# Duo attention and a weighted sum of experts: keys head by head, expert weights in halves, first products earlier

## The chip, the cores and the metric

The kernel runs on one core of one Trainium2 chip. A core has TensorE (PE in the profile; its weight loads are PEld), VectorE (DVE), ScalarE (ACT), GpSimd (POOL) and SyncE (SP). Each takes its own instructions in order; they wait for each other through semaphores. DMA queues are filled from SP, ACT and POOL. The metric is the device time of one execution in microseconds, the median over runs.

## The reference

Eight heads of attention over 4 batches of 768 positions, then four experts over the 3072 rows that come out. Three heads (0, 2, 6) see all earlier keys ("retrieval"); five (1, 3, 4, 5, 7) see the first 4 keys and the last 64 ("streaming").

```python
scores = scale * np.matmul(q, k.transpose(0, 1, 3, 2))
stream_keep = causal & (is_sink | in_win)        # n_sink 4, window 64
mask = np.where(retr, causal, stream_keep)
a = softmax(np.where(mask, scores, -1e9))
x = matmul(a, v)                                 # to [N = 3072, D = 512]
p = domain_probs / (domain_probs.sum(-1, keepdims=True) + 1e-09)
for e in range(E):                               # E = 4, F = 1024
    h = np.maximum(x @ w1[e], 0.0)
    out += p[:, e:e + 1] * (h @ w2[e])
```

## The kernel before

**Stages.** Attention goes in 8 groups of 384 positions: group g is batch g // 2, half g % 2. What a group gives lies transposed in `xT[g]` (128 x 4 x 384: four quarters of the 512 inputs). The experts go over 24 token tiles of 128 rows. Tiles 0 to 2 (group 0) and then tile 3 take the plain way (`plain_steps`): for each expert, layer 1 makes 8 feature tiles, each a sum of four products (one for each quarter of the inputs, in the order 1, 0, 2, 3), which ACT takes out of PSUM with Relu (L1161); layer 2 makes for each token tile a sum of 8 products with `w2sb` (L1169), which DVE takes out times the probability (L1181, L1185). The other 20 tiles go in pairs (`pair_steps`) with Winograd's scheme, which needs sums of the weights and of the inputs; the sums of the inputs (`x_sum`) lie in the part of the key buffer that the windows of the later batches leave free.

**Order.** All engines' orders are written out by hand. `attention(0, 0)` runs first and alone. Then `moe_steps` yields steps, and after each one a plan decides by a running count whether the next steps of the following attention group are to be put in. `plan[1]` says from when group 1 is put in, in units of the plain work of one expert on group 0 (`UNIT`). Semaphore waits between instructions are put in by the layer that records them.

**Group 0's attention.** In it PE transposes keys and queries of a pair of heads (L619), DVE copies the keys into `kR` (retrieval, L645) or `kS` (streaming, L661, and the four first keys into every tile, L669), PE makes the scores (L736, biases L748), ACT the exponentials (L754), PE the values (L799, L863, and for the pairs 1, 5 and 3, 7 L905), and ACT and DVE divide by the sums (L914, L915, L918, L884, L828). The order is: transposes of heads 0, 1; scores 0, 1; transposes of 4, 5; values 0; scores 4, 5; transposes of 2, 3; values 1, 5; scores 3; transposes of 6, 7; and so on. `warm_up` puts matmuls on zeros where PE would wait; `WARM` says how many.

**Streaming keys.** `kS` holds 8 tiles of 96 keys with room for 128, for 5 heads. Before, the order within a partition is half, tile, head, key (`c t s x`). In later batches it holds 7 windows per head instead (`windows(kSf)`, L281), and what lies behind them holds `x_sum`. The two halves are zeroed at the start, the first by DVE, the second by POOL (both L371).

**POOL's start.** POOL builds masks, requests some of the values, casts values to 16 bits (L432), waits until the queries have landed (`landed`, L552), requests expert 0's first weights (`load_w1`, L327: two requests, one for each half of the partitions), casts again, requests expert 0's second weights (`load_w2`, L349), casts, zeroes the second half of the retrieval and of the streaming keys, fills in ones, and goes on with the next weights and with group 1's keys, queries and values. Requests of POOL are counted on eight semaphores in turn, so each waits for the eighth before it to land.

**PSUM.** `bank()` deals out four buffers in turn for scores, transposes and layer 1 (`pA`); `pO` has two for layer 2, and `pV` two.

Of the kernel before, what the change touches and what calls it, by code (L numbers as in the profile page):

```python
# [11 lines left out]
FP32 = mybir.dt.float32  # L12
# [7 lines left out]
def kernel(  # L20
# [42 lines left out]
    DMP = DM // P  # L63
    FTP = F // P
    NTILE = N // P
    G = B * NCH
# [5 lines left out]
    SH = [h for h in range(H) if not RETR[h]]  # L72
# [5 lines left out]
    NT = S // TK  # L78
    TC = CH // TK
# [3 lines left out]
    WT = 7  # L83
# [14 lines left out]
    gp = nc.gpsimd  # L98


    def bank():
        return pA.tile([P, 512], FP32, name="pA", bufs=4)
# [20 lines left out]
    kSf = pers.tile([P, NT * NSH * P], FP16, name="kS")  # L123
    vSf = pers.tile([P, NT * NSH * P], FP16, name="vS")

    kS = kSf.rearrange("p (c t s x) -> p c t s x", c=NCH, t=TC, s=NSH)
    vS = vSf.rearrange("p (c t s x) -> p c t s x", c=NCH, t=TC, s=NSH)

    def windows(x):

        return x[:, 0 : WT * NSH * P].rearrange("p (t s x) -> p t s x", t=WT, s=NSH)
# [36 lines left out]
    def half(u):  # L168
        return slice(u * D, (u + 1) * D)
# [8 lines left out]
    def key_tile(b, c, h, t):  # L178

        i = b % 2  # L180
        if RETR[h]:
            return kR[i][:, t // 3, RH.index(h), t % 3, :]
        if b:
            return windows(kSf)[:, t, SH.index(h), :]
        return kS[:, t // TC, t % TC, SH.index(h), :]

    def v_tiles(b, c, h):
# [90 lines left out]

    def keys_to_windows(b, c, part):

        x = windows(kSf)  # L281
        for r, n0, hp0, n in [((1, 0, 0, 2), (1, 3, 2, 2), (0, 2, 2, 1))[part]]:
            r = half(r)
            src = kT[r, hp0 : hp0 + n, P - WO + NS :]
            step = src.ap[1][0]
            src = bass.AP(
                src.tensor, src.offset, [src.ap[0], [step, n], [WQ, WT], [1, P - NS]]
            )
            dst = x[r, :, n0 : n0 + n, :].rearrange("p t n x -> p n t x")
            nc.vector.tensor_copy(out=dst[:, :, :, NS:P], in_=src)  # L290
            if c == 0:
                src = kT[r, hp0 : hp0 + n, P : P + NS]
                src = src.rearrange("p n (t x) -> p n t x", t=1)
                nc.vector.tensor_copy(
                    out=dst[:, :, :, 0:NS], in_=src.to_broadcast([D, n, WT, NS])
                )
        if part == 2 and b * NCH + c + 1 < G:
            nc.vector.tensor_copy(out=kT[:, :, P - WO : P], in_=kT[:, :, CH + P - WO :])
# [22 lines left out]
                out=vS[0:NS, c, t, :, :], in_=vS[R0 : R0 + NS, 0, 0, :, :]  # L321
            )

    def load_w1(e, f0, f1):
        x = moe_w1[e].rearrange("(u c d) f -> u d c f", u=2, c=DMP)
        for u in range(2):
            gp.dma_start(  # L327
                out=w1sb[half(u), e * DMP : (e + 1) * DMP, f0:f1],
                in_=x[u, :, :, f0:f1],
            )  # L330
# [14 lines left out]

    def load_w2(e):
        x = w2sb[:, e * FTP : (e + 1) * FTP, :]
        if in_pairs(e):
            gp.dma_start(  # L349
                out=x.rearrange("p (m j) d -> p m (j d)", j=2),  # L350
                in_=moe_w2[e].rearrange("(m p j) d -> p m (j d)", p=P, j=2),
            )
            return
        gp.dma_start(out=x, in_=moe_w2[e].rearrange("(fo fi) d -> fi fo d", fi=P))


    ONES = 0.0078125 * (1.0 + 15360.0 * 2.0**-23)

# [2 lines left out]
    def fill(eng, ap, value):  # L361
        ap = ap.bitcast(FP32)
        if eng is nc.scalar:
            src = ones[0 : ap.shape[0], :]
            if len(ap.shape) == 3:
                src = src.rearrange("p (a b) -> p a b", a=1)
            elif len(ap.shape) == 4:
                src = src.rearrange("p (a b c) -> p a b c", a=1, b=1)
            eng.copy(out=ap, in_=src.to_broadcast(list(ap.shape)))
        else:  # L370
            eng.memset(ap, value)  # L371

    def zero(eng, t):
        fill(eng, t.rearrange("p a b x -> p (a b x)"), 0.0)
# [60 lines left out]
    for n, h in enumerate(ORDER0):  # L435
# [24 lines left out]
        out=probs,  # L460
# [8 lines left out]
    make_identity(nc, ident32)  # L469
    one_values(nc.vector, 0)  # L470
    zero(nc.vector, kR[0][:, 0, :, :, :])
    zero(nc.vector, kS[:, 0, :, :, :])
    nc.vector.tensor_copy(out=ident16, in_=ident32)


# [76 lines left out]
        gp.tensor_copy(out=seen, in_=x)  # L552

    def w1_of(e):
        return w1sb[D : D + 1, e * DMP, 0:1]


    def w2_of(e):
        return w2sb[0:1, e * FTP, 0:1]


    landed(q32[0:1, 0, 6, 0:1])
    load_w1(0, 0, F)
    cast_v(gp, (4, 2, 3, 6))
    load_w2(0)
    cast_v(gp, (7,))
    zero(gp, kR[0][:, 1, :, :, :])
    zero(gp, kS[:, 1, :, :, :])
    one_values(gp, 1)

    load_w1(1, 0, F)
    landed(w1_of(0))
    load_triples(k, k16, 0, 1, 0, HP)
    load_triples(q, qt16, 0, 1, 0, HP)
# [2 lines left out]
    landed(qt16[0:1, 0, 0, 0:1])  # L577
    load_triples(k, k16, 0, 1, HP, H)
    load_triples(q, qt16, 0, 1, HP, H)
    load_w1(2, 0, F)  # L580
# [6 lines left out]
    load_w1(3, 0, F)  # L587
    load_w2(3)
    assert E == 4
    mSf = mS.rearrange("p t x -> p (t x)")  # L590
# [5 lines left out]

    def mm_ns(cols):
        return cols / 2.4 + 2.5

    def attention(b, c):  # L600
        g = b * NCH + c
# [320 lines left out]
            later(scale, g)  # L922
            yield 800.0

        WARM = {("s", 0): 3, ("v", 1): 3, ("v", 3): 4, ("v", 2): 2, ("v", 6): 2}

        def both(a, bb):

# [11 lines left out]
        if first:  # L940
# [190 lines left out]
    def acc_of(nt):  # L1131
        n0 = 2 * FTP * CH + nt * 2 * DM if nt < 3 else 5 * KT * P - 2 * DM
        return hA[:, n0 : n0 + 2 * DM].bitcast(FP32)

    def plain_steps(nt0, tiles, e, tokens, n0):

        cols_n = tiles * P
        hs = hA[:, n0 : n0 + FTP * cols_n].rearrange("p (f x) -> p f x", f=FTP)
        require(nt0 // 3)
        x = tokens()  # L1140
        ahead = 4 if nt0 == 0 and e == 0 else 1
        for f0 in [0, *range(ahead, FTP)]:
            pss = {ft: bank() for ft in range(f0, f0 + (1 if f0 else ahead))}
            cts = (1, 0, 2, 3)

            def layer1(ft, n):
                ct = cts[n]
                nc.tensor.matmul(  # L1148
                    out=pss[ft][:, 0:cols_n],
                    lhsT=w1_tile(e, ct, ft),  # L1150
                    rhs=x[:, ct, :],
                    start=(n == 0),
                    stop=(n == DMP - 1),
                )

            for ft in pss:
                for n in range(DMP - 1):
                    layer1(ft, n)
            for ft, ps in pss.items():
                layer1(ft, DMP - 1)  # L1160
                nc.scalar.activation(  # L1161
                    out=hs[:, ft, :], in_=ps[:, 0:cols_n], func=AF.Relu
                )
                yield DMP * mm_ns(cols_n), 0.6
        for j in range(tiles):
            nt = nt0 + j
            ps_o = pO.tile([P, DM], FP32, name="pO", bufs=2)
            for ft in range(FTP):
                nc.tensor.matmul(  # L1169
                    out=ps_o,  # L1170
                    lhsT=hs[:, ft, j * P : (j + 1) * P],
                    rhs=w2sb[:, e * FTP + ft, :],
                    start=(ft == 0),
                    stop=(ft == FTP - 1),
                )
                if ft == FTP // 2 - 1:
                    yield FTP // 2 * mm_ns(DM), 1.4
            p_ap = p_sb[:, nt, e : e + 1]
            if e == 0:
                acc[nt] = acc_of(nt)  # L1180
                nc.vector.tensor_scalar(  # L1181
                    out=acc[nt], in0=ps_o, scalar1=p_ap, scalar2=None, op0=ALU.mult
                )
            else:
                nc.vector.scalar_tensor_tensor(  # L1185
                    out=acc[nt], in0=ps_o, scalar=p_ap, in1=acc[nt],
                    op0=ALU.mult, op1=ALU.add,
                )
            if e == E - 1:
                nc.sync.dma_start(out=out[nt * P : (nt + 1) * P, :], in_=acc[nt])  # L1190
            yield FTP // 2 * mm_ns(DM), 1.4
# [46 lines left out]
        return scaled(e)[:, j * KH : (j + 1) * KH, i * P : (i + 1) * P]  # L1238

    second_set = set()  # L1240

    def x_sum(e, n):
# [31 lines left out]
    def pair_steps(nt0, nxt):  # L1274
# [446 lines left out]
```

## Time and profile before

| what | value |
|---|---|
| time, median of 3 runs | 376.75 us (376.45 to 376.91) |
| time of the profiled execution | 376.67 us |
| its span | 374.9 us |
| mean granted clock of PE | 0.998 |
| PE, DVE, ACT, POOL busy | 364.9, 278.1, 226.5, 113.7 us |
| expert 0's layer 1 on group 0 starts | 20.79 us |
| expert 0's layer 2 on group 0 | 26.23 to 31.57 us |
| tile 3's plain work starts | 72.73 us |

The span runs from the first instruction to the last; the time of the execution holds 1.77 us more around it. Rows of a timeline give start, duration, engine, line, operation, what is written and read, how many were merged, and in brackets how long the engine was idle before it and for what. Durations of merged rows reach from the first start to the last end. Rows of waits give the total, how often, and the longest. Line numbers are those of the kernel before.

### The profile page before, as it was taken

How to read it: one execution, taken by the hardware profiler on the slowest of the kernel's cores; microseconds unless marked ns; L12 is line 12 of the kernel's file. 1: busy time of each engine (PE TensorE's matmuls, PEld its weight loads, DVE VectorE, ACT ScalarE, POOL GpSimd, SP SyncE). 2: the span in 40 equal slices, each digit the busy share in tenths (PEclk: the TensorE clock that was granted, in tenths of full speed). 3: DMA queues.
4: the chain of work that ended last, by engine and by line, in shares of the span. 5: the costliest groups of instructions: out<-in, count | busy, mean ns of one | idle time of the engine just before them, and what ended most of it. 6: DMA issues, size and time to landing. Idle time of an engine off the chain costs nothing.

```text
span 374.9 us, 10308 instructions
## 1 busy us (share of the span) xinstructions
PE 364.9 (97%) x4219; PEld 310.2 (83%) x4219; DVE 278.1 (74%) x583; ACT 226.5 (60%) x471; POOL 113.7 (30%) x162
## 2 busy tenths in 40 slices
PE   7889899999999999999999999999999999999996
PEld 4645466678998988999989899988899998998995
DVE  5765867798687679868657858857768868979881
ACT  5644579547786785775776856774777361451630
POOL 8844573872067039015501640220000000000000
PEclk9999999999999999999999999999999999999999
DMA  9999999999799399989905990951220300300101
GB/s 179 193 211 206 195 195 182 180 201 97 111 104 163 79 99 139 156 96 85 187 2 73 166 152 12 140 121 12 72 68 2 111 7 2 114 3 14 43 3 58
DMA packets 122340, 39.65 MB, mean 106 GB/s; under 512 B 112192, under 2 KB 114820, under 8 KB 122292
## 3 DMA queue, kind: packets, MB, share of 16 engines
q0 software_dynamic: 82816, 19.01, 57.6%
q1 hardware_dynamic: 37876, 19.58, 23.5%
q8 instruction: 33, 0.54, 0.6%
q10 hardware_dynamic: 1600, 0.39, 0.5%
q14 instruction: 15, 0.12, 0.1%
HBM read 44.89 MB, written 6.34 MB: 137 GB/s over the span
## 4 chain that ended last, share of the span: by engine, by line
PE 85%; DVE 6%; DMA 5%; POOL 1%; issue 1%; ACT 1%; POOLq 0%; DVEq 0%
PE pO L1462 29%; PE pA L1282 21%; PE pO L1311 9%; PE pA L1148 7%; PE pO L1169 7%; PE pA L736 4%; DMA w1sb<-in_moe_w_dram 2%; PE pV L1311 2%; PE pA L1311 2%; PE pV L799 2%; DVE xs L1233 2%; PE pV L863 2%; DMA xT<-x_pair 1%; DMA hA<-in_v_dram 1%; DVE hA L1067 1%
## 5 line engine op out<-in xcount | busy, mean ns | idle before, releaser
L1462 PEld LDWEIGHTS <-hA 128*128 128x128 f16 x1104 | 104.8, 98 | 11.9
L1282 PE MATMUL pA<-xs,w1sb 128*128 128x256 f16 x768 | 97.1, 272 | 0.0
L1282 PEld LDWEIGHTS <-w1sb 128*128 128x128 f16 x768 | 71.7, 98 | 7.3
L1462 PE MATMUL pO<-w2sb,hA 128*128 128x256 f16 x640 | 76.8, 272 | 0.0
L754 ACT ACTIVATE es<-pA 128x384 f16<-128x384 f32 (+2 forms) x122 | 59.0, 512 | 27.4 <-PE pA L736 22.5
L1291 ACT ACTIVATE hA<-pA 128x512 f16<-128x512 f32 x96 | 57.2, 598 | 29.4 <-PE pA L1282 27.2
L306 POOL DMA_DIRECT2D vS<-in_v_dram x30 | 29.6, 988 | 111.7 <-PE pV L863 110.2
L1462 PE MATMUL pO<-tsb,hA 128*128 128x256 f16 x464 | 56.8, 272 | 0.0
L1233 DVE TENSOR_TENSOR xs<-xT,pB 128x1024 f16<-128x1024 f16 (+1 forms) x49 | 47.0, 977 | 2.9 <-DMA xT<-x_pair 2.9
L1067 DVE TENSOR_TENSOR hA<-hA 128x1024 f16<-128x1024 f16 x60 | 39.4, 685 | 0.6 <-PE pO L1462 0.3
L1161 ACT ACTIVATE hA<-pA 128x384 f16<-128x384 f32 (+1 forms) x64 | 22.2, 385 | 20.3 <-PE pA L1148 20.0
L1311 PEld LDWEIGHTS <-w1sb 128*128 128x128 f16 x512 | 31.3, 98 | 1.9 <-DVE xs L1067 0.6
L1148 PE MATMUL pA<-xT,w1sb 128*128 128x384 f16 (+1 forms) x256 | 30.4, 273 | 1.3 <-DMA w1sb<-in_moe_w_dram 1.2
L1169 PE MATMUL pO<-w2sb,hA 128*128 128x512 f16 x128 | 30.6, 379 | 0.0
L1482 ACT COPY s<-pO 128x256 f32<-128x256 f32 x31 | 11.6, 373 | 27.3 <-PE pO L1462 21.8
L1148 PEld LDWEIGHTS <-w1sb 128*128 128x128 f16 x256 | 19.4, 98 | 10.1 <-issue 1.7
L765 DVE TENSOR_TENSOR es<-es,mS 128x384 f16<-128x384 f16 (+1 forms) x40 | 13.8, 344 | 17.9 <-ACT es L754 17.9
L884 DVE TENSOR_TENSOR xT<-pV,rc 64x384 f16<-64x384 f32 x36 | 20.0, 555 | 8.3 <-ACT rc L881 7.7
L1328 DVE CUSTOM_DVE_ANT_0 hA<-pO,s 128x512 f16<-128x512 f32 x26 | 17.7, 688 | 9.8 <-PE pO L1311 8.5
L878 ACT ACTIVATE rc<-pV,eps 64x384 f32<-64x384 f32 x36 | 20.7, 576 | 6.6 <-PE pV L863 6.0
L1321 ACT COPY s<-pO 128x512 f32<-128x512 f32 x39 | 22.7, 587 | 3.2 <-PE pO L1311 3.0
L736 PE MATMUL pA<-qT,kR 128*128 128x128 f16 (+2 forms) x141 | 23.1, 261 | 0.7 <-DVE kR L645 0.7
(175 smaller groups left out, 520.3 us busy)
## 6 DMA issues: line engine op xcount, KB each, us to landing
pB<-p_rows SPq DMA_DIRECT2D x10, 512.0 KB
out_dram<-o SPq DMA_DIRECT2D x19, 256.0 KB
w1sb<-in_moe_w_dram POOLq DMA_DIRECT2D x8, 512.0 KB, 9.0
w2sb<-in_moe_w_dram POOLq DMA_DIRECT2D x4, 1024.0 KB, 11.3
vS<-in_v_dram POOLq DMA_DIRECT2D x30, 112.0 KB, 4.6
k_rows<-in_k_dram POOLq DMA_DIRECT2D x18, 128.0 KB, 5.0
q<-in_q_dram POOLq DMA_DIRECT2D x18, 128.0 KB, 6.0
out_dram<-hA SPq DMA_DIRECT2D x4, 256.0 KB
```

Source lines behind the costliest of these rows:

```text
L306: gp.dma_start(out=t[:, :, own_v(h)], in_=windows_of(v, b, h, c))
L736: nc.tensor.matmul(out=ps[:, o : o + nq], lhsT=key_tile(b, c, h, t), rhs=qTs[b, c][:, hp, q0 : q0 + nq], start=(n == 0 or not first), stop ...
L754: nc.scalar.activation(out=es[:, 0:cols], in_=ps[:, 0:cols], func=AF.Exp, scale=SC)
L1067: nc.vector.tensor_tensor(out=out, in0=a, in1=b, op=ALU.subtract)
L1148: nc.tensor.matmul(out=pss[ft][:, 0:cols_n], lhsT=w1_tile(e, ct, ft), rhs=x[:, ct, :], start=(n == 0), stop=(n == DMP - 1),)
L1169: nc.tensor.matmul(out=ps_o, lhsT=hs[:, ft, j * P : (j + 1) * P], rhs=w2sb[:, e * FTP + ft, :], start=(ft == 0), stop=(ft == FTP - 1),)
L1233: nc.vector.tensor_tensor(out=o, in0=xin, in1=pb.to_broadcast([P, DMP, n, P]), op=ALU.mult)
L1282: nc.tensor.matmul(out=ps[:, f * PC : (f + 1) * PC], lhsT=w1_tile(e, ct, f0 + f), rhs=xs[:, ct, :], start=(ct == 0), stop=(ct == DMP - 1),)
L1291: nc.scalar.activation(out=blocks[:, b0 : b0 + 2, k0 : k0 + 2, :].rearrange("p t f x -> p f t x"), in_=ps.rearrange("p (f t x) -> p f t x" ...
L1311: nc.tensor.matmul(out=ps[:, f * P : (f + 1) * P], lhsT=w_tile(e, w[:, ct, :], f), rhs=a[:, ct, :], start=(first and f == 0 and ct == 0), ...
L1321: nc.scalar.copy(out=kept[n], in_=ps)
L1462: nc.tensor.matmul(out=ps, lhsT=a[:, k, :], rhs=b(k), start=(first and k == 0), stop=(k == KT - 1), skip_group_check=not first,)
```

## The change

- The streaming keys lie head by head: the order within a partition is head, half, tile, key (`s c t x`). The windows of later batches are a view of the same order (`kW`), whose eighth tile of each head holds `x_sum` until all attention is done (`after_keys`), as two runs of 128 with other keys between; before the third last pair's second layer `require(G - 1)` asks for the attention to be finished, and from there on `x_sum` goes where it went before. The zero fill of a half is five runs (`zero_keys`).
- `load_w1` makes four requests (two quarters of the inputs, one half of the partitions each) in place of two, and `load_w2` two in place of one. What `landed` looks at lies in the last of them.
- Layer 1 of the plain experts makes the products of the first two quarters for four feature tiles ahead, for every expert on group 0 (before: for expert 0 alone, with three quarters ahead). Of expert 0 the first two feature tiles' first products are made in group 0's attention (`begin_products`), ahead of the values of heads 3 and 7, where four warm-up matmuls were.
- Layer 2 on group 0 goes over halves of the features: first half of tile 0, first half of tile 1, second half of 0, second half of 1, then both of tile 2.
- Group 1 is put in from 1.2 units on (before: 1.06).

```diff
-    kS = kSf.rearrange("p (c t s x) -> p c t s x", c=NCH, t=TC, s=NSH)
+    kS_rows = kSf.rearrange("p (s c t x) -> p c s t x", c=NCH, t=TC, s=NSH)
+    kS = kS_rows.rearrange("p c s t x -> p c t s x")
+    kW = kSf.rearrange("p (s t x) -> p t s x", s=NSH, t=NT)
...
-            return windows(kSf)[:, t, SH.index(h), :]
+            return kW[:, t, SH.index(h), :]
...
-        x = windows(kSf)
+        x = kW[:, 0:WT, :, :]
...
-    def load_w1(e, f0, f1):
+    def load_w1(e):
         x = moe_w1[e].rearrange("(u c d) f -> u d c f", u=2, c=DMP)
-        for u in range(2):
-            gp.dma_start(
-                out=w1sb[half(u), e * DMP : (e + 1) * DMP, f0:f1],
-                in_=x[u, :, :, f0:f1],
-            )
+        for c in range(0, DMP, 2):
+            for u in range(2):
+                gp.dma_start(
+                    out=w1sb[half(u), e * DMP + c : e * DMP + c + 2, :],
+                    in_=x[u, :, c : c + 2, :],
+                )
...
     def load_w2(e):
         x = w2sb[:, e * FTP : (e + 1) * FTP, :]
-        if in_pairs(e):
+        for n in range(2):
+            if in_pairs(e):
+                m = slice(n * FTP // 4, (n + 1) * FTP // 4)
+                gp.dma_start(
+                    out=x.rearrange("p (m j) d -> p m (j d)", j=2)[:, m, :],
+                    in_=moe_w2[e].rearrange("(m p j) d -> p m (j d)", p=P, j=2)[
+                        :, m, :
+                    ],
+                )
+                continue
+            m = slice(n * FTP // 2, (n + 1) * FTP // 2)
             gp.dma_start(
...
+    def zero_keys(eng, c):
+        fill(eng, kS_rows[:, c, :, :, :].rearrange("p s t x -> p s (t x)"), 0.0)
...
-    zero(nc.vector, kS[:, 0, :, :, :])
+    zero_keys(nc.vector, 0)
...
-        return w1sb[D : D + 1, e * DMP, 0:1]
+        return w1sb[D : D + 1, (e + 1) * DMP - 1, 0:1]
...
-    zero(gp, kS[:, 1, :, :, :])
+    zero_keys(gp, 1)
...
+    def begin_products(e, fts):
+
+        for ft in fts:
+            begun[0, e, ft] = bank()
+            layer1(begun[0, e, ft], e, ft, xT[0], (0, 1))
...
-        WARM = {("s", 0): 3, ("v", 1): 3, ("v", 3): 4, ("v", 2): 2, ("v", 6): 2}
+        WARM = {("s", 0): 3, ("v", 1): 3, ("v", 2): 2, ("v", 6): 2}
...
             yield from values(6)
+            begin_products(0, (0, 1))
             yield from values_pair(3, 7)
...
-        ahead = 4 if nt0 == 0 and e == 0 else 1
+        ahead = 4 if nt0 == 0 else 1
         for f0 in [0, *range(ahead, FTP)]:
...
+            for ft in range(f0, f0 + (1 if f0 else ahead)):
+                if (nt0, e, ft) in begun:
+                    pss[ft] = begun.pop((nt0, e, ft))
+                    continue
+                pss[ft] = bank()
+                layer1(pss[ft], e, ft, x, (0, 1))
+            if nt0 == e == f0 == 0:
+                for ft, ps in pss.items():
+                    layer1(ps, e, ft, x, (2,))
             for ft, ps in pss.items():
-                layer1(ft, DMP - 1)
+                layer1(ps, e, ft, x, (3,) if nt0 == e == f0 == 0 else (2, 3))
...
-        for j in range(tiles):
+        FH = FTP // 2
+        parts = [(j, n) for j in range(tiles) for n in range(2)]
+        if nt0 == 0:
+            parts = [(0, 0), (1, 0), (0, 1), (1, 1), (2, 0), (2, 1)]
+        sums_of = {}
+        for j, n in parts:
             nt = nt0 + j
-            ps_o = pO.tile([P, DM], FP32, name="pO", bufs=2)
-            for ft in range(FTP):
+            if n == 0:
+                sums_of[j] = pO.tile([P, DM], FP32, name="pO", bufs=2)
+            ps_o = sums_of[j]
+            for ft in range(n * FH, (n + 1) * FH):
...
     def x_sum(e, n):
 
+        if not after_keys:
+            return kW[:, WT, n * KH : (n + 1) * KH, :]
...
+        if nt0 == pairs[-3]:
+            require(G - 1)
+            after_keys.append(True)
...
-    plan = {1: (1.06 * UNIT, 3.5 * UNIT)}
+    plan = {1: (1.2 * UNIT, 3.5 * UNIT)}
```

More of the change, by code (lines that the diff above doesn't have):

```diff
@@ L124 @@
     vSf = pers.tile([P, NT * NSH * P], FP16, name="vS")
-    kS = kSf.rearrange("p (c t s x) -> p c t s x", c=NCH, t=TC, s=NSH)
+    kS_rows = kSf.rearrange("p (s c t x) -> p c s t x", c=NCH, t=TC, s=NSH)
+    kS = kS_rows.rearrange("p c s t x -> p c t s x")
+    kW = kSf.rearrange("p (s t x) -> p t s x", s=NSH, t=NT)
+    assert NT == WT + 1
     vS = vSf.rearrange("p (c t s x) -> p c t s x", c=NCH, t=TC, s=NSH)
@@ L347, in load_w2 @@
         x = w2sb[:, e * FTP : (e + 1) * FTP, :]
-        if in_pairs(e):
+        for n in range(2):
[9 more added lines that the diff above has]
+            m = slice(n * FTP // 2, (n + 1) * FTP // 2)
             gp.dma_start(
-                out=x.rearrange("p (m j) d -> p m (j d)", j=2),
-                in_=moe_w2[e].rearrange("(m p j) d -> p m (j d)", p=P, j=2),
-            )
-            return
-        gp.dma_start(out=x, in_=moe_w2[e].rearrange("(fo fi) d -> fi fo d", fi=P))
+                out=x[:, m, :],
+                in_=moe_w2[e].rearrange("(fo fi) d -> fi fo d", fi=P)[:, m, :],
+            )
     ONES = 0.0078125 * (1.0 + 15360.0 * 2.0**-23)
@@ L554, in w1_of @@
     def w1_of(e):
-        return w1sb[D : D + 1, e * DMP, 0:1]
+        return w1sb[D : D + 1, (e + 1) * DMP - 1, 0:1]
     def w2_of(e):
-        return w2sb[0:1, e * FTP, 0:1]
+        return w2sb[0:1, (e + 1) * FTP - 1, 0:1]
     landed(q32[0:1, 0, 6, 0:1])
-    load_w1(0, 0, F)
+    load_w1(0)
     cast_v(gp, (4, 2, 3, 6))
@@ L567 @@
     zero(gp, kR[0][:, 1, :, :, :])
-    zero(gp, kS[:, 1, :, :, :])
+    zero_keys(gp, 1)
     one_values(gp, 1)
-    load_w1(1, 0, F)
+    load_w1(1)
     landed(w1_of(0))
@@ L579 @@
     load_triples(q, qt16, 0, 1, HP, H)
-    load_w1(2, 0, F)
+    load_w1(2)
     load_v(0, 1, RH)
@@ L586 @@
     landed(w1_of(2))
-    load_w1(3, 0, F)
+    load_w1(3)
     load_w2(3)
@@ L1133, in acc_of, with layer1 @@
         return hA[:, n0 : n0 + 2 * DM].bitcast(FP32)
+    CTS = (1, 0, 2, 3)
+    begun = {}
+    def layer1(ps, e, ft, x, ns):
+        for n in ns:
+            nc.tensor.matmul(
+                out=ps[:, 0 : x.shape[2]],
+                lhsT=w1_tile(e, CTS[n], ft),
+                rhs=x[:, CTS[n], :],
+                start=(n == 0),
+                stop=(n == DMP - 1),
+            )
     def plain_steps(nt0, tiles, e, tokens, n0):
@@ L1140, in plain_steps @@
         x = tokens()
-        ahead = 4 if nt0 == 0 and e == 0 else 1
+        ahead = 4 if nt0 == 0 else 1
         for f0 in [0, *range(ahead, FTP)]:
[L1143 to L1158, printed above, removed]
+            pss = {}
+            for ft in range(f0, f0 + (1 if f0 else ahead)):
[7 more added lines that the diff above has]
+                    layer1(ps, e, ft, x, (2,))
             for ft, ps in pss.items():
-                layer1(ft, DMP - 1)
+                layer1(ps, e, ft, x, (3,) if nt0 == e == f0 == 0 else (2, 3))
                 nc.scalar.activation(
@@ L1175, in plain_steps @@
                 )
-                if ft == FTP // 2 - 1:
-                    yield FTP // 2 * mm_ns(DM), 1.4
+            if n == 0:
+                yield FH * mm_ns(DM), 1.4
+                continue
             p_ap = p_sb[:, nt, e : e + 1]
@@ L1240 @@
     second_set = set()
+    after_keys = []
     def x_sum(e, n):
+        if not after_keys:
+            return kW[:, WT, n * KH : (n + 1) * KH, :]
         n0 = (2 * P * 8 if e in second_set else WT * NSH * P) + n * KH * P
```

## The prediction, made before the changed kernel was run

> **What bounds the kernel now.** I read first the page's totals, then the chain of waits, then the timelines of TensorE (PE), VectorE (DVE) and GpSimd (POOL) over the first 60 us, because every edit but two acts there.
>
> ```profile
> span 374.9 us, 10308 instructions
> PE 364.9 (97%) x4219; PEld 310.2 (83%) x4219; DVE 278.1 (74%) x583; ACT 226.5 (60%) x471; POOL 113.7 (30%) x162
> PE 85%; DVE 6%; DMA 5%; POOL 1%; issue 1%; ACT 1%; POOLq 0%; DVEq 0%
> ```
>
> PE is busy 97% of the span and makes 85% of the chain. From about 47 us to the end it has no wait over 0.3 us, so a microsecond won or lost in group 0 is still there at the end. The 10 us in which PE is idle lie almost all ahead of 47 us, and these are the two that the change aims at:
>
> ```profile
> PE pA L1148 <- DMA w1sb<-in_moe_w_dram: 1.2, 1, 1.2
> PE pA L736 <- DVE kS L661: 1.1, 1, 1.1
> ```
>
> The first is the wait for expert 0's first weights at 20.79 us; the second, at 46.52 us, is a score of group 1 that waits for another head's key copy. Now the work of group 0 around the key copies, and POOL beside it:
>
> ```profile
> 6.40 0.56 DVE L661 CAST kS<-pA 64x384 f16<-64x384 f32 x1
> 8.52 0.55 DVE L661 CAST kS<-pA 64x384 f16<-64x384 f32 x1 [1.47 <-PE pA L619]
> 9.21 0.31 PE L736 MATMUL pA<-qT,kS 128*128 128x160 f16 x2 [0.54 <-DVE kS L669]
> 11.01 0.18 POOL L552 CAST seen<-hA 1x1 f16<-1x1 f32 x1 [0.63 <-DMA hA<-in_q_dram]
> 11.13 1.25 POOL L327 DMA_DIRECT2D w1sb<-in_moe_w_dram  x2
> 14.35 0.76 POOL L349 DMA_DIRECT2D w2sb<-in_moe_w_dram  x1
> 15.44 0.60 POOL L371 MEMSET kR<- 128x576 f32 x1
> 15.96 1.19 POOL L371 MEMSET kS<- 128x1280 f32 x1
> 19.20 0.34 PE L845 MATMUL pV<-ident,x_pair 128*128 128x128 f16 x3
> 20.79 5.61 PE L1148 MATMUL pA<-xT,w1sb 128*128 128x384 f16 x32 [1.25 <-DMA w1sb<-in_moe_w_dram]
> ```
>
> The reader should see that DVE copies head 1's keys at 6.40 and head 4's at 8.52, and that POOL zeroes the second half of the streaming keys only at 15.96 to 17.15, behind a wait for the queries (11.01), the issue of expert 0's weights and four casts. Before the change nobody in group 0 waits for that fill.
>
> **The change, part by part.**
>
> *Keys head by head.* The zero fill of one half of the keys was one run of 1280 words; now it is five runs of 256, one per head, with the other half's runs between them. I read the built programs of both kernels engine by engine with their waits. In the changed one the second key copy of group 0 on DVE (head 4, at 8.52 before) waits for PE's transpose, as before, and also for POOL's 25th counted instruction. That is the zero fill of the other half. PE's first weight load from head 4's keys (9.21) has the same wait. In the program before, POOL's 25th is first asked for by DVE and PE in group 1. The bytes don't meet, but head 4's copy lies between the first and the last byte of the five runs; head 1's, ahead of them, has no such wait. So the layout takes the false wait of group 1 away and puts one into group 0.
>
> When does the fill end? POOL runs on, as nothing it does until then waits for PE or for head 4. Expert 0's first weights are now four requests of 64 x 2 rows in place of two of 64 x 4, which took 0.62 us each. POOL's other requests (96 x 4 rows 0.69, 128 x 4 rows 0.76, 128 x 8 rows 0.90) say that rows cost little beside a base, so I take 0.58 for 64 x 2 (0.5 to 0.62): 4 x 0.58 = 2.3 in place of 1.25, ending at 13.5. The casts after it had waited 0.24 + 0.28 us for values that have now landed, and end at about 14.8 rather than 14.4. The second weights are two requests of 128 x 2 rows, 0.69 each (0.62 to 0.76), in place of one of 0.76: 16.2 where 15.11 was. So the fill ends at 17.15 + 1.05 = 18.2 us (17.7 to 18.5).
>
> DVE's copy then starts at about 18.27 in place of 8.52: **+9.75 us** (9.2 to 10.1). Behind it on DVE stand head 5's copy, the division of head 0's values and all later copies of group 0; behind PE's own wait all scores from head 4 on; ACT waits for those scores. Nothing of this can run ahead, as each engine goes in order, and from 8.52 to 19.54 these three wait for each other: in PE's waits there I find no DMA and no POOL wait that the delay would absorb. So the end of group 0 moves by the whole.
>
> *PE's clock after the gap.* PE finishes head 0's values at about 8.7 and then stands until 18.97, some 10.2 us. No gap of before is longer than 1.3 us, so no row shows what follows. The nearest is the start of the program, where PE also comes from standing:
>
> ```profile
> 1.67 0.15 PEld L480 LDWEIGHTS <-early 128*128 128x128 f16 x1 [0.28 <-issue]
> 2.09 0.15 PEld L480 LDWEIGHTS <-early 128*128 128x128 f16 x1 [0.28 <-issue]
> 26.23 5.34 PE L1169 MATMUL pO<-w2sb,hA 128*128 128x512 f16 x24
> ```
>
> The first eight matmuls of 512 columns follow each other at 0.42 to 0.43 us, for 3.6 us; later ones at 5.18 / 24 = 0.216 (31.41 less 26.23 over 24). I take it that PE goes at half rate again for about as long. Then heads 4 and 5's scores, 2 x 1152 columns, take 1.92 us in place of 0.96; of this, 0.5 is hidden, as PE waited there for DVE anyway (9.89 and 10.69). The transposes (0.65), the small ones (0.16) and 768 columns of warm-up (0.32) double up to where 3.6 us are full: another 0.6. Together **+1.1 us**; nothing if the clock stays, 2.2 if it takes twice as long to come back.
> [...]
>
> *Weights in halves, first products ahead.* Before, PE stood from 19.54 to 20.79 for the weights. With group 0 late by 10 us they (20.65) and the second weights (25.52 at the latest) have long landed, so using halves alone wins nothing more. Four products of 384 columns (0.65 us) replace four warm-ups of 256 (0.43) ahead of values(3, 7), which moves those by 0.28 against the scores they waited for (18.51). In times of before: the transposes end at 19.8, the last quarter of the inputs comes at 21.3 (L918 ended at 21.04), and only that quarter's product is left, 0.16, then the drain 0.17, ACT 0.50 and 0.04: the fifth feature tile starts at 22.25. Before it did at 23.64. **-1.4 us** (-1.2 to -1.5).
>
> *Layer 2 in halves.* The sum of the first token tile now ends four matmuls (0.86 us) ahead of the third's start in place of eight (1.73), and two PSUM buffers serve three tiles. DVE took 0.75 us for a tile and began 0.20, 0.26 and once 0.67 after PE's end: 0.20 + 0.75 + 0.05 is 0.14 too late, up to 0.6. It counts for experts 0 and 3; for 1 and 2 scores and values of group 1 lie between. **+0.3** (0 to 1.5).
>
> *Four tiles ahead for experts 1 to 3, and group 1 from 1.2 units.* Four PSUM banks are now wanted at once. In expert 2 they include those of heads 6 and 7's transposes, so PE there waits for the same DVE copies (46.46) as the 1.1 us wait of before, with less work ahead: 43.10 to 46.46 less four products of layer 2 (0.86), two scores (0.22) and four of layer 1 (0.65) leaves 1.6, against 1.14. In expert 3 they wait for ACT's exponentials. I take **+0.4**, from -1.1 (the old wait gone) to +1.
>
> *At nothing:* twelve more requests and their shorter lanes: transfers stay in one order, never fewer than some 1.5 MB ahead, and the 10 us cover what comes later; without that cover one request late is 0.6 us. The sums' new place (two runs of 128 on DVE in place of one of 256), and the last requirement: beyond expert 3, PE, DVE and ACT have the same instructions in the same order.
>
> Sum, against the profiled execution's 376.67 us (span 374.9 and 1.77 around it, 0.08 below the median of 376.75): +9.75 + 1.1 - 1.4 + 0.3 + 0.4 = +10.15, so **386.8 us**.
>
> **Rivals.**
>
> *The same wait, the clock kept.* The transposes after the gap run as before: 386.8 - 1.1 = 385.7. For it: the granted clock reads 1.00 even in the first slice. Against: that slice has the half-rate matmuls all the same.
>
> *The same wait and more behind it:* half rate twice as long (+1.1) and banks and PSUM buffers late in every expert (+2): 390. For it: ACT and DVE are near full between 56 and 68 us. Against: these stretches held PE up by 1.1 us in all.
>
> *Not slower.* The false wait is met, or is no wait on the chip, so group 0 keeps its time, and the halves win what they are for: the first half of the weights lands half a transfer ahead, (1.05 MB / 2) / 211 GB/s = 2.5 us, at 18.2, PE goes on without its 1.25 us wait, the fifth tile starts at 22.4 in place of 23.64, and 0.7 - 1.1 goes for banks: about 375. It decides only if the fill is done by 8.5 + 1.25 = 9.8 us; POOL asks for the weights ahead of the fill, and not before 11.01.
>
> **How the numbers follow.** Forecast 0.72, clock kept 0.15, more behind 0.09, not slower 0.04. The range goes from 376.67 + 9.2 + 0 - 1.4 - 1.1 = 383.4 to 376.67 + 10.1 + 2.2 - 1.2 + 2 = 389.8, rounded to 390. About 0.2% (0.75 us) is what a measurement of this kernel can tell from no change. All but the last rival are slower by over 2%: slower 0.96; the last gives faster 0.025, same 0.015.
>
> **What would show it.** In the changed profile: DVE's second key copy at about 18.3, idle some 9.7 us before it and put down to POOL's fill of the keys; PE idle about 10 us ahead of head 4's scores; matmuls of heads 4 and 5 at about twice their spacing; the first product of layer 1 with no wait for a DMA; short waits of PE for DVE at the third token tile. The forecast is wrong if POOL's fill stands well ahead of 17 us, or if PE has no gap near 9 us.

## The result and the profile after

| what | before | after |
|---|---|---|
| time, median | 376.6 us (376.38 to 376.91, 4 runs) | 390.32 us (389.29 to 390.99, 4 runs) |
| time of the profiled execution | 376.67 us | 389.79 us |
| mean granted clock of PE | 0.998 | 0.982 |

The changed kernel takes 1.0361 times as long (95% interval 1.0333 to 1.039): it is slower, and by 0.3 us slower than the upper end of the range that was predicted (two of its four executions, 389.29 and 389.79 us, lie inside). First the page of the kernel after: its totals, the chain that ended last, and the granted clock in 40 slices.

```profile
span 388.0 us, 10318 instructions
PE 367.4 (95%) x4215; PEld 311.4 (80%) x4215; DVE 277.6 (72%) x583; ACT 226.0 (58%) x471; POOL 119.8 (31%) x174
PE 88%; DVE 3%; ACT 2%; POOL 2%; DMA 2%; SPq 1%; issue 1%; ACTq 0%
PEclk9579999999999999999999999999999999999999
```

The span grew by 13.1 us and PE's busy time by 2.5: most of the loss is time in which PE stands. A little of it is time in which PE goes slowly, as the second and third digit of the clock (5 and 7, both 9 before) say. The timeline of the kernel after shows where it stands (start, duration, engine, line, operation, tiles; in brackets the idle time ahead and its releaser):

```profile
6.04 0.56 DVE L681 CAST kS<-pA 64x384 f16<-64x384 f32 x1
11.20 2.40 POOL L331 DMA_DIRECT2D w1sb<-in_moe_w_dram  x4
14.84 1.43 POOL L355 DMA_DIRECT2D w2sb<-in_moe_w_dram  x2
17.10 1.21 POOL L382 MEMSET kS<- 128x1280 f32 x1
18.34 0.55 DVE L681 CAST kS<-pA 64x384 f16<-64x384 f32 x1 [11.64 <-POOL vR L382]
19.12 0.43 PE L756 MATMUL pA<-qT,kS 128*128 128x160 f16 x2 [10.77 <-DVE kS L689]
29.67 0.34 PE L819 MATMUL pV<-vR,es 128*128 128x65 f16 x6
31.40 5.37 PE L1161 MATMUL pA<-xT,w1sb 128*128 128x384 f16 x28
36.61 5.48 PE L1204 MATMUL pO<-w2sb,hA 128*128 128x512 f16 x24
86.31 1.95 PE L1161 MATMUL pA<-xT,w1sb 128*128 128x128 f16 x32
```

Head 4's keys, copied at 8.52 before, are copied at 18.34, just behind POOL's fill of the other half of the keys (17.10 + 1.21 = 18.31). The bracket names `vR`, the fill that POOL begins next at 18.21 and that takes 0.15, across the start of the copy. PE stands 10.77 us for that copy. The four requests for the first weights took 0.60 each and the two for the second 0.715. Layer 1 of expert 0 now starts without a wait for a DMA.

The loss can be read off in steps, by how much later each landmark is than before:

| landmark | before | after | later by | step |
|---|---|---|---|---|
| DVE's copy of head 4's keys | 8.52 | 18.34 | 9.82 | +9.82 |
| values of head 6 (L799, now L819) | 17.86 | 29.67 | 11.81 | +1.99 |
| layer 2 of expert 0 | 26.23 | 36.61 | 10.38 | -1.43 |
| layer 1 of expert 1 | 31.41 | 41.93 | 10.52 | +0.14 |
| tile 3's plain work | 72.73 | 86.31 | 13.58 | +3.06 |
| last matmuls of the span | 369.78 | 382.88 | 13.10 | -0.48 |

The values of head 6 are the last work of PE in group 0 that the new place of the first products does not move. Their row in the timeline of the kernel before:

```profile
17.86 0.34 PE L799 MATMUL pV<-vR,es 128*128 128x65 f16 x6
```

Two large steps besides the first put the time up. From the copy of head 4's keys to these values it is 9.34 us before and 11.33 after: the same work takes 1.99 us longer. That is the clock; the windows of the kernel after show it (start and end, length, busy us and instructions of PE, PEld, DVE, ACT and POOL, granted clock, DMA share, GB/s):

```profile
10.50:11.00 0.50, 0.00 (x0) 0.00 (x0) 0.00 (x0) 0.00 (x0) 0.00 (x0) 0.73 1.02 157
11.00:11.50 0.50, 0.00 (x0) 0.00 (x0) 0.00 (x0) 0.00 (x0) 0.42 (x2) 0.50 1.33 207
23.50:24.00 0.50, 0.50 (x8) 0.30 (x8) 0.49 (x2) 0.00 (x0) 0.50 (x1) 0.50 1.09 205
24.00:24.50 0.50, 0.50 (x16) 0.50 (x12) 0.38 (x2) 0.00 (x0) 0.19 (x1) 0.62 1.15 217
24.50:25.00 0.50, 0.50 (x13) 0.37 (x8) 0.00 (x0) 0.26 (x1) 0.00 (x0) 1.00 1.11 205
```

The clock falls to a half at about 10.73 us (0.73 of full speed over half a microsecond), 2.4 us after PE's last matmul of head 0's values ended at 8.35, and comes back at about 24.38: PE works 5.26 us at half rate, from 19.12.

The other is the stretch of experts 1 to 3, with group 1's attention put in. Before, its one wait over 0.3 us was the 1.14 us for a key copy. The timeline of PE in the kernel after, rows with a wait there:

```profile
56.84 1.15 PE L1161 MATMUL pA<-xT,w1sb 128*128 128x384 f16 x6 [0.56 <-DVE kS L681]
58.63 0.32 PE L756 MATMUL pA<-qT,kR 128*128 128x384 f16 x1 [0.64 <-ACT hA L1189]
59.53 0.33 PE L756 MATMUL pA<-qT,kS 128*128 128x64 f16 x3 [0.58 <-ACT es L774]
60.94 0.27 PE L756 MATMUL pA<-qT,kS 128*128 128x160 f16 x2 [0.22 <-ACT es L774]
75.51 0.33 PE L756 MATMUL pA<-qT,kS 128*128 128x64 f16 x3 [0.55 <-ACT hA L1189]
78.47 0.81 PE L1161 MATMUL pA<-xT,w1sb 128*128 128x384 f16 x4 [0.61 <-ACT hA L1189]
```

In two of these rows scores (L756) wait for ACT's Relu of a feature tile (`hA`, L1189): the two share nothing but the four PSUM banks. In two others scores wait for ACT's exponentials of earlier scores (`es`), and in two layer 1 (L1161) waits for a key copy and for a Relu. The six waits are 3.16 us. Each also costs the drain of a matmul, by estimate about 0.17 us (a row of two matmuls of 384 columns lasts 0.49 where two take 0.32 in a stream), 1.0 in all. Less the old wait of 1.14 with its drain, that is 2.9 of the 3.06 us.

### The profile page after: what moved, and what is told of

Read it like the earlier page. It is cut to its first block, busy times and chain, and to the rows that moved or that the text cites. A ratio compares the mean times of both kernels' runs of the same rounds, so it can differ in the third digit from the quotient of the medians.

```text
span 388.0 us, 10318 instructions
## 1 busy us (share of the span) xinstructions
PE 367.4 (95%) x4215; PEld 311.4 (80%) x4215; DVE 277.6 (72%) x583; ACT 226.0 (58%) x471; POOL 119.8 (31%) x174
## 4 chain that ended last, share of the span: by engine, by line
PE 88%; DVE 3%; ACT 2%; POOL 2%; DMA 2%; SPq 1%; issue 1%; ACTq 0%
PE pO L1504 30%; PE pA L1321 22%; PE pO L1350 9%; PE pA L1161 6%; PE pO L1204 6%; PE pA L756 5%; PE pV L1350 2%; PE pV L819 2%; PE pA L1350 2%; PE pV L883 2%; DMA hA<-in_q_dram 2%; DVE xs L1269 1%; ACT es L774 1%; DVE kS L681 1%; ACT hA L1189 1%
## 5 line engine op out<-in xcount | busy, mean ns | idle before, releaser
L1189 ACT ACTIVATE hA<-pA 128x384 f16<-128x384 f32 (+1 forms) x64 | 21.9, 386 | 21.2 <-PE pA L1161 19.9
L1161 PE MATMUL pA<-xT,w1sb 128*128 128x384 f16 (+1 forms) x256 | 31.6, 272 | 1.3 <-ACT hA L1189 0.6
L756 PE MATMUL pA<-qT,kS 128*128 128x56 f16 (+4 forms) x255 | 16.6, 196 | 12.1 <-DVE kS L689 10.8
L1161 PEld LDWEIGHTS <-w1sb 128*128 128x128 f16 x256 | 19.2, 98 | 10.2 <-issue 1.7
L756 PEld LDWEIGHTS <-kS 128*128 128x128 f16 x255 | 13.2, 98 | 15.8 <-POOL vR L382 10.9
L756 PE MATMUL pA<-qT,kR 128*128 128x128 f16 (+2 forms) x141 | 23.2, 261 | 1.7 <-DVE kR L665 0.8
```

The source lines that it names most:

```text
L756: nc.tensor.matmul(out=ps[:, o : o + nq], lhsT=key_tile(b, c, h, t), rhs=qTs[b, c][:, hp, q0 : q0 + nq], start=(n == 0 or not first), stop ...
L1161: nc.tensor.matmul(out=ps[:, 0 : x.shape[2]], lhsT=w1_tile(e, CTS[n], ft), rhs=x[:, CTS[n], :], start=(n == 0), stop=(n == DMP - 1),)
L1189: nc.scalar.activation(out=hs[:, ft, :], in_=ps[:, 0:cols_n], func=AF.Relu)
```

## The experiments

Each was timed against the kernel before on its own chip; ratios are to it.

**Five separate fills.** POOL's fill of a half is five instructions of 256 words, each within one head, in place of one with five runs. Theory A: the fill's span makes the wait.

```diff
-        fill(eng, kS_rows[:, c, :, :, :].rearrange("p s t x -> p s (t x)"), 0.0)
+        for s in range(NSH):
+            fill(eng, kS_rows[:, c, s, :, :].rearrange("p t x -> p (t x)"), 0.0)
```

> The changed kernel with POOL's zero fill of the second half of the streaming keys as five instructions, one for each head, in the same place of POOL's queue and over the same bytes. Theory A (the one fill spans the other half's runs, so that head 4's key copy waits for it; PE then also loses its clock): DVE's second key copy is back at about 8.2 us, PE has no gap near 9 us, the granted clock is 1.00, and the time falls by the 9.9 us of the gap and some 1.8 us of clock, to 377.8 us (376.5 to 379); what is left over the kernel before is the stalls in group 1, less the wait for the first weights. Rival B (the delay comes from the smaller requests on POOL, or from the layout itself): the gap stays and the time stays at 390 us.

Measured: 378.73 us, ratio 1.0056 (1.0043 to 1.007). The timeline of this kernel, DVE's second key copy and POOL's fill:

```profile
8.63 0.55 DVE L682 CAST kS<-pA 64x384 f16<-64x384 f32 x1 [1.48 <-PE pA L640]
...
17.86 1.34 POOL L382 MEMSET kS<- 128x256 f32 x5
```

The fill is even later than before, and the copy no longer waits for it, only for PE's transposes. The same bytes are filled by the same engine at the same place in its queue; all that differs is that no single instruction reaches across another head's keys. That is worth 11.6 us, the clock's part with it. The waits in group 1 stayed as they were.

**Only one tile ahead for experts 1 to 3.** Tried with the one fill and with the five:

```diff
-        ahead = 4 if nt0 == 0 else 1
+        ahead = 4 if nt0 == 0 and e == 0 else 1
```

> The changed kernel, fill as it is, with four feature tiles begun ahead for expert 0 alone. Theory C: group 0 keeps its gap, experts 1 to 3 lose most of the 3.2 us of PE's waits, and the time falls by 2 to 3.5 us, to 387.4. Rival D: no change within 0.7 us, 390.

> As five_fills, and four feature tiles are begun ahead for expert 0 alone, as in the kernel before. Theory C (four PSUM banks taken at once hold up PE in experts 2 and 3: the scores that lie between wait for ACT to take out a tile just finished): PE's waits for ACT and DVE between experts 1 and 3, 3.2 us in the changed kernel, mostly go, and the time is 2 to 3.5 us below five_fills, some 374.8 us. Rival D (the later start of group 1, 1.2 units, or layer 2 in halves makes those waits): within 0.7 us of five_fills.

With the one fill it took 386.65 us, ratio 1.0264 (1.0247 to 1.028), 3.7 us less than the changed kernel (3.1 between the two profiled executions), and tile 3's work began at 82.49 rather than 86.31. With five fills it took 375.26 us, ratio 0.9962 (0.9949 to 0.9975): 3.5 us less than with five fills and four ahead (3.0 between the profiled executions), and faster than the kernel before. Its list of waits has none of a score for `hA` or of layer 1 for `kS` any more. One new wait has come, in its timeline:

```profile
45.51 0.48 PE L1162 MATMUL pA<-xT,w1sb 128*128 128x384 f16 x2 [1.07 <-DMA w1sb<-in_moe_w_dram]
```

PE reaches expert 2 earlier, and its weights' second half isn't there.

**Two tiles ahead.** Is it the split of the products that costs, or that all four banks are taken? Five fills, and:

```diff
-        ahead = 4 if nt0 == 0 else 1
+        ahead = (4 if e == 0 else 2) if nt0 == 0 else 1
```

> Five fills, and two tiles ahead for experts 1 to 3 in place of four (four for expert 0). Theory C1 (what four ahead cost is that the next score, put between two feature tiles, gets the bank of the feature tile just made, as the four banks are dealt in turn, and so waits for its Relu): with two, the bank of the next score has been free for long, the waits for ACT's hA and es go, and the time is that of one ahead: 375.3 us (374.8 to 375.9). Rival C2 (the cost is in the split of the products, and goes with how many are ahead): a third of 3.5 us is left, 376.4.

Measured: 375.12 us, ratio 0.9972 (0.9962 to 0.9982), without a wait for ACT in the stretch; 0.51 us of the new wait for expert 2's weights is left. Theory C1 holds: with two tiles ahead the next bank in turn has long been free; with four it is that of the feature tile just made.

**PE kept busy in the gap.** The changed kernel with 44 matmuls of 512 columns on zeros where PE stands:

```diff
             yield from values(0)
+            warm_up(ps_warm, 44, 512)
             yield from scores(4)
```

> The changed kernel with 44 more warm-up matmuls of 512 columns (44 x 0.216 = 9.5 us) between head 0's values and head 4's scores, so that PE works through the time in which DVE waits for POOL. Theory E (the gap costs the clock as well): DVE's second key copy still starts at 18.3 us, but heads 4 and 5's scores run at full rate, the granted clock is 1.00 to 24 us and the time falls by 1.5 to 2.0 us, to 388.6. Rival F (the slower start after the gap is only waiting for other engines): the time stays at 390.3 within 0.5 us.

Measured: 388.39 us, ratio 1.0313 (1.0294 to 1.0331), so 1.9 us less than the changed kernel (2.1 between the profiled executions). First PE's and DVE's rows in the timeline of this kernel, then its window behind the gap, with the clock in the third column from the end:

```profile
8.96 9.66 PE L494 MATMUL pO<-early 128*128 128x512 f16 x44
18.27 0.55 DVE L681 CAST kS<-pA 64x384 f16<-64x384 f32 x1 [10.76 <-POOL vR L382]
19.05 0.30 PE L756 MATMUL pA<-qT,kS 128*128 128x160 f16 x2 [0.42 <-DVE kS L689]
27.61 0.34 PE L819 MATMUL pV<-vR,es 128*128 128x65 f16 x6
```

```profile
19.00:21.00 2.00, 1.83 (x18) 1.33 (x19) 1.45 (x6) 1.32 (x4) 1.94 (x5) 1.00 1.12 211
```

The copy is as late as ever and head 4's scores begin at about the same time, yet the clock stays at 1.00 and a score row takes 0.30 instead of 0.43. From the copy to the values of head 6 it is 9.34 us again (18.27 to 27.61), as in the kernel before, where the changed kernel takes 11.33. What is won is the price of the clock. In two of the four executions the mean clock was 1.00 (387.65 and 387.85 us), in the other two 0.996 (388.94 and 389.08 us); these were not traced, so the 1.9 us of the medians is, if anything, too little.

**The layout alone.** The kernel before with only the keys head by head (views, sums of the inputs, fill), without halves, first products, layer 2 or the new plan; once with one fill of five runs for a half, once with five fills:

```diff
-    kS = kSf.rearrange("p (c t s x) -> p c t s x", c=NCH, t=TC, s=NSH)
+    kS_rows = kSf.rearrange("p (s c t x) -> p c s t x", c=NCH, t=TC, s=NSH)
+    kS = kS_rows.rearrange("p c s t x -> p c t s x")
...
-    zero(gp, kS[:, 1, :, :, :])
+    zero_keys(gp, 1)
```

> Theory A (the key layout alone carries the long wait, through the one fill that spans head 4's region): in the kernel before, POOL's fill of the second half ends at 17.15 us, so DVE's second key copy comes at about 17.2 instead of 8.52, +8.7; PE's clock after the gap +1.8; the weights' wait (1.25) is hidden by the delay, -1.25; group 1's wait of 1.14 for head 7's copy is gone, -1.1. Together +8.1: 384.6 us (383.3 to 386). Rival (the long wait comes from the weights' requests in pieces on POOL, and the layout is harmless): 375 to 377 us, with the key copy at 8.5.

> Theory F (the layout with five separate fills is all gain: group 1's wait of 1.14 us at 46.5 goes, as head 7's copy no longer seems to touch other heads' keys): 375.4 us (375.0 to 375.8), PE's list of waits without the 1.1 for DVE's key copy. Rival (the copy is needed there anyway, or another wait takes its place): 376.4 to 376.8. Group 0 goes as in the kernel before in both.

One fill: 385.9 us, ratio 1.0245 (1.0227 to 1.0263); five: 376.35 us, ratio 0.9988 (0.9979 to 0.9997). The timeline of the first of the two:

```profile
16.17 1.19 POOL L373 MEMSET kS<- 128x1280 f32 x1
17.39 0.55 DVE L666 CAST kS<-pA 64x384 f16<-64x384 f32 x1 [10.48 <-POOL kS L373]
18.17 0.42 PE L741 MATMUL pA<-qT,kS 128*128 128x160 f16 x2 [9.63 <-DVE kS L674]
```

So the layout alone carries the long wait (theory A; the time lies in its range, 1.3 us above its sum), and the requests in halves only put the fill off by another microsecond (17.36 to 18.31, its end). Theory F was mostly a miss. Group 1's wait of 1.14 us is gone as it says, but waits of 0.23 (a key copy) and 0.32 (layer 1, for a bank) stand in its place, and of the 1.35 us expected 0.3 to 0.4 are left: the rival's mechanism. The one fill also shows two prices alone. From head 4's copy to the values of head 6 it takes 10.48 us (17.39 to 27.87) where the kernel before takes 9.34: the clock costs 1.14 us here. And from these values to layer 2 of expert 0 it takes 7.45 us (27.87 to 35.32) where the kernel before takes 8.37: 0.92 us comes back without any halves or first products, because the weights have landed by then (layer 1 waits 0.32 us for DVE there and for no DMA).

**What the other parts are worth without the two stalls.** From the version with five fills and one tile ahead (375.26 us), one part at a time was undone: the first products ahead of the last values; layer 2 in halves; the new plan.

```diff
-            begin_products(0, (0, 1))
...
-        WARM = {("s", 0): 3, ("v", 1): 3, ("v", 2): 2, ("v", 6): 2}
+        WARM = {("s", 0): 3, ("v", 1): 3, ("v", 3): 4, ("v", 2): 2, ("v", 6): 2}
```

> This is the version with five fills and four tiles ahead only for expert 0 (375.26), without the first products ahead of group 0's last values, and with the four warm-up matmuls back there. Theory G (those products are work that fills a stretch in which PE would wait or warm up): layer 1 starts at about 19.7 with all 32 products, 0.65 us of matmuls come back and 0.28 of warm-ups' delay goes, expert 0's layer 2 starts at about 25.4 instead of 25.02: 375.65 us. Rival (the weights' halves alone carry the gain): 375.2. Rival (the last half of the weights is the limit, about 20.8): 375.3 to 375.5.

```diff
-            parts = [(0, 0), (1, 0), (0, 1), (1, 1), (2, 0), (2, 1)]
+            parts = [(0, 0), (0, 1), (1, 0), (1, 1), (2, 0), (2, 1)]
```

> The version with five fills and four tiles ahead only for expert 0 (375.26), with layer 2 again tile by tile. Theory H (halves of layer 2 only cost: the third tile's PSUM buffer comes 0.14 late at experts 0 and 3, and the second half of the weights has landed anyway): 375.0 us (374.7 to 375.2), layer 2 of expert 0 in 5.34 rather than 5.54 us. Rival (the second half of the second weights lands after 25.9, so the whole order waits for it): a DMA wait of up to 0.5 us for w2 and 375.3 to 375.8.

```diff
-    plan = {1: (1.2 * UNIT, 3.5 * UNIT)}
+    plan = {1: (1.06 * UNIT, 3.5 * UNIT)}
```

> Five fills, four tiles ahead only for expert 0, and group 1 put in from 1.06 units again (1.2 in the changed kernel). Theory P (the wait of 1.07 us for the second half of expert 2's weights stands because less of group 1 lies ahead of it): with one step more of group 1 ahead of expert 2 the wait falls by 0.3 to 0.8 us, 374.5 to 375.0. Rival (the start of group 1 is then the wait, for its keys and queries that land at about 33.0): 375.3 to 375.8.

Without the first products: 375.23 us, ratio 0.9961 (0.9948 to 0.9975), no difference. From the values of head 6 to layer 2 of expert 0 it takes 6.96 us (18.28 to 25.24), with them 6.94 (18.08 to 25.02), so theory G fell. The time is the first rival's. The other rival, that the last half of the weights is the limit, is shown in part: with the first products PE waits for the weights in group 0, 0.29 us in the trace with five fills and four ahead and 0.25 in that with layer 2 by whole tiles; without them no such wait is in the trace. Layer 2 by whole tiles: 375.24 us, ratio 0.9961 (0.9947 to 0.9974), no difference either; expert 0's layer 2 takes 5.34 in place of 5.54, but its lead has gone by the end, within what can be measured, and the 375.0 us of theory H was not reached. With group 1 from 1.06 units: 375.99 us, ratio 0.9992 (0.9982 to 1.0002), 0.7 us more by the medians and 1.1 by the ratios, which come from two chips. Theory P fell. The wait for expert 2's weights is gone there, and the start of group 1 waits for its queries (0.41 us), with 0.33 for a bank and 0.24 for a key copy later: the rival's mechanism, and a little more than its time.

Last, the version without first products, its weights in whole requests again:

```diff
-        for c in range(0, DMP, 2):
-            for u in range(2):
+        for u in range(2):
...
-        for n in range(2):
+        for n in range(1):
```

> The version without the first products ahead (375.23) with its weights in whole requests again (two for the first, one for the second). Theory W (the halves win what they let start early): PE waits again about 1.2 us ahead of layer 1 of expert 0, which starts at 20.8 in place of 19.79, and expert 0's second layer at 26.3 rather than 25.24: +1.0, of which some 0.5 is given back where the weights of expert 2 are waited for: 375.75 us (375.4 to 376.3). Rival (twelve requests fewer let all later transfers start earlier, and expert 2's weights come without a wait): 374.9 to 375.3.

Measured: 376.46 us, ratio 1.0009 (0.9999 to 1.002), 1.2 us more by the medians and 0.0048 (1.8 us) more by the ratios, which come from two chips. PE waits for the weights ahead of layer 1 again, as the timeline of this kernel shows:

```profile
20.57 1.14 PE L1160 MATMUL pA<-xT,w1sb 128*128 128x384 f16 x6 [0.49 <-DMA w1sb<-in_moe_w_dram]
```

In the profiles the way from the values of head 6 to layer 2 of expert 0 is 0.66 us longer (18.40 to 26.02, 7.62 against 6.96): the wait and its drain. So the halves win what they are for, once nothing else stands ahead of it. The time lies a little above the range of theory W, and the wait is shorter than the 1.2 us it named, mostly because the values of head 6 come at 18.40 in this profile and at 17.86 in the kernel before, which waits 1.25 us; the later group 0 is, the less of the wait is left. The rest of the 1.1 us between the two profiles is spread: 0.12 ahead of these values, 0.12 from layer 2 to tile 3, 0.21 behind tile 3.

## Why the prediction was too low

By its own steps:

- *The false wait in group 0*: right in its place, its releaser and its size. Forecast 9.75 us, with the copy at 18.27 and the fill's end at 18.2; measured 9.82, 18.34 and 18.31. Five fills remove it.
- *PE's clock after the gap*: right in that the clock fell to a half (0.50 of full speed from 11.00 to 24.00), size too small. Forecast 1.1 (0 to 2.2); the landmarks say 1.99, the run with PE kept busy 1.9. The step that failed in it is "for about as long" as at the start of the program, 3.6 us. The price for such a time was right: in the layout alone 3.21 us of work at half rate cost 1.14. But in the changed kernel it was 5.26, and the heads' scores, the transposes of the next heads, the warm-ups and the values of 1 and 5 all fell into it.
- *Weights in halves, first products ahead*: forecast -1.4, measured -1.43. That was for a group 0 which is 10 us late, and by the layout alone 0.92 of it comes from the delay; the 0.51 left over is, by estimate, what the two edits won. With group 0 on time the first products are worth nothing, and the halves at least 0.66 us.
- *Layer 2 in halves*: 0.14 at expert 0 as worked out; the 0.3 for the whole kernel was not separated.
- *Four tiles ahead for experts 1 to 3, and group 1 from 1.2 units*: this is the term that was mis-sized, and it put the time above the range. Forecast "+0.4, from -1.1 [...] to +1"; measured +3.06 by the landmarks, and by undoing the four tiles 3.5 to 3.7 in the medians and 3.0 to 3.1 in the profiles. The forecast priced one wait in expert 2, when the four banks are first taken, at 1.6 in place of 1.14; that wait was in truth 0.56. For the rest it said only that in expert 3 they "wait for ACT's exponentials", with nothing in the sum. But the banks go round in turn, so a score put between two feature tiles gets the bank of the one just made and stands until its Relu is done, and what follows waits for the banks behind it. That comes again and again within a group of four, with the drain each time: 0.64, 0.58 and 0.22 in expert 2, 0.55 and 0.61 in expert 3 (these two for a Relu, not for exponentials). The plan was no part of the loss as far as is known: with five fills and one tile ahead 1.2 units is the better of the two by 0.7 us.
- From tile 3 to the end 0.48 us came back, where nothing was forecast. The version with five fills and one tile ahead takes as little there (296.57 us from tile 3 to the last matmuls, 297.05 before). The layout alone does not do it (297.25 and 297.08), and the changed kernel with one tile ahead takes 297.39; which edit does it stays open.
- *The working*: the upper end of the range takes +2 for layer 2 and the banks, where their own upper bounds, 1.5 and 1, make 2.5; with these the range would have ended at 390.3. And of the 10 us in which PE is idle before, 3.2 lie behind the last matmul (371.73 to 374.9), not ahead of 47 us.

The rivals: the clock was not kept. The second one, half rate for longer (+1.1) and banks late in every expert (+2), given 0.09, comes to 390 us; its two parts are what the runs found, the clock's somewhat less and the banks' somewhat more, though only in experts 2 and 3. Not slower: with five instructions for the fill the long wait is gone, but the time is 378.73 us, 0.6% above the kernel before; its "about 375" needs fewer tiles ahead as well (375.26).

## What to carry to other kernels

Here the layer that puts in the waits took one fill of five runs for all that lies between its first and last byte: head 4's copy came at 18.34 us, and at 8.63 with five fills. When a layout turns one run into several, look at what lies between them, and write one instruction for each run. Taking all four buffers of a ring at once cost 3.0 to 3.7 us here, where other work of that ring is put in between; two of four did as well as one. What an edit is worth depends on which wait ends last there: the halves and the first products together won some 0.5 us in a group 0 that came 10 us late, and on time the halves alone won at least 0.66 and the first products nothing. Of the versions run, four stand at 375.1 to 375.3 us, 0.3 to 0.4% faster than the kernel before; from the changed kernel, five fills with one or two tiles ahead for experts 1 to 3 is all it takes.

## What the runs showed of the clock

In three traces the clock changed at different times behind PE's last matmul before the gap and its first one after it. In the kernel after it fell 2.4 us after PE's last matmul and came back 5.26 us after the first; in the layout alone with one fill it fell at about 11.14, 2.6 us after PE's last matmul (8.54), and came back at 21.38, only 3.2 us after PE began again at 18.17. In the changed kernel with one tile ahead it fell 4.3 us after the last matmul (9.23 to 13.56; the window from 13.50 to 14.00 has 0.56) and came back at 23.80 (0.70 in that from 23.50 to 24.00), 4.6 us after PE began again at 19.19. The windows of the layout alone, granted clock in the third column from the end:

```profile
11.00:11.50 0.50, 0.00 (x0) 0.00 (x0) 0.00 (x0) 0.00 (x0) 0.25 (x2) 0.64 1.33 191
...
21.00:21.50 0.50, 0.50 (x5) 0.50 (x4) 0.29 (x1) 0.00 (x0) 0.50 (x2) 0.62 1.08 205
21.50:22.00 0.50, 0.50 (x7) 0.38 (x5) 0.44 (x1) 0.00 (x0) 0.50 (x1) 1.00 1.17 221
```

From fall to return it is 13.65 us in the kernel after, 10.24 in this one, and 10.24 in the changed kernel with one tile ahead. What sets these lengths is not shown by the runs. In this order 5.26, 3.21 and 4.61 us of them lie behind the gap, as work at half rate, and cost 1.99, 1.14 and 1.68 us up to the values of head 6; the forecast's 1.1 was worked out for 3.6 us of it. The executions of one kernel differ in it: the mean granted clock of the kernel after was 0.982 in three executions and 0.987 in the fastest one, which is by estimate 14 and 10 us at half rate ((1 - 0.982) x 388 / 0.5 and (1 - 0.987) x 387.6 / 0.5).
